# The sign of a float64 weight carried in the exponent through a parametric ReLU

## The chip, the cores and the metric

The program runs on one core of a Trainium2 chip. Its engines work side by side, each through its own queue in program order: TensorE (PE: matmuls, with PEld for the weight loads), VectorE (DVE), ScalarE (ACT), GpSimd (POOL), and SyncE (SP), which here issues DMA transfers. The metric is the device time of one execution in microseconds; lower is better.

## The reference

The program computes attention with a learned relative-position bias (2 x 8 heads, 576 positions, 64 wide), and then two dense blocks on the 1152 resulting rows of 512 numbers. Cut to what matters here:

```python
attn_out = _attn_ref(q, k, v, w1, b1, w2)
x = attn_out.transpose(0, 2, 1, 3).reshape(B * S, H * D)
h = x @ w_in                                   # block 1: 512 -> 2048
g = P(h) / (Q(h) + 1e-06)                      # P cubic, Q quadratic in |h|
x = g @ w_out                                  # 2048 -> 512
h = x @ w_in2                                  # block 2, other weights
g = where(h >= 1, h, where(h <= -1, 0, (h + 1)**2 / 4))
return (g @ w_out2).astype(float32)
```

The four weight matrices of the two blocks arrive as float64.

## The kernel before

PE multiplies fp32 numbers that are split in two: a high part (`wh`, `xh`, `gh`) and the remainder (`wl`, `xl`, `gl`), three matmuls for one product. So each float64 weight is turned into an fp32 word on the core, and that word into a high and a low part. This is `conv` (L475). It works on 64 tiles of 128 x 512 float64 numbers, 32 of queue k = 0 (the `w_in` side, pool `raw0`, results `wh` and `wl`) and 32 of queue k = 1 (the `w_out` side, pool `raw1`, result `wo`), in five stages, one per step:

- s0: `wc` = the high 32 bits, read as fp32, times 2^-112 (`copy`, L135 on ACT or L145 on POOL, whichever the planner takes).
- s1: two instructions. On ACT the top byte of the low word, shifted right by five bits through an arithmetic Copy on bytes, replaces the lowest byte of the high word in `raw` (L500; it is called the octet copy below). On DVE `wc` is shifted left by 3 bits (L501), which sets the exponent right and drops the sign.
- s2: DVE takes the sign and the low three bits from the high word in `raw` and joins them to `wc` (L504).
- s3: the next load into this `raw` buffer is issued on SP (`w_load`, L474; two buffers per queue, and the load waits until s2 has read the old content), and the high part is copied (L135 on ACT, L139 on DVE or L145 on POOL).
- s4: the low part is a subtraction on DVE or POOL (L150).

Four `wc` buffers rotate. Thirteen of the 64 conversions are placed in the attention stage, at steps that the table names (`ready0`: 27, 33, 37, 54, 69, 73; `ready1`: 59, 64, 67, 70, 73, 75, 77); the others stand in the dense blocks, eight for each twelve steps at first.

The order of the instructions is made when the program is built. A step is a row of operations with priorities; those that may run on several engines carry a cost for each, and `pick` (L100) gives each to the engine whose planned load stays lowest. So a changed cost or a removed choice moves other flexible operations too: the high-part copies, the first writes of `acc` (L139 or L135) and the additions into it, which run on DVE (L650) or as a copy to `dr` on ACT and an addition on POOL (L655).

In the attention stage a step holds the scores (L365, PE), their reduction with the bias (L374, DVE), the exponential (L379, ACT), the normalisation (L147, mostly POOL), transposes (L405, PE), their copies to `PT` (L135, ACT) and the product with V (L418 and L421, PE), from which `xh` (L438, ACT) and `xl` (L440, DVE) are made. In block 1 PE makes `inps` (L692), ACT and DVE turn it into `v` (L557 to L590), ACT and POOL split it into `gh` and `gl` (L594, L598), and nine steps later PE makes `outps` (L735). Between the blocks the sum `acc` is split into `x2h` (L667, ACT) and `x2l` (L668, DVE), which block 2 multiplies.

Of the kernel before, what the change touches and what calls it, by code (L numbers as in the profile page):

```python
# [8 lines left out]
AF = mybir.ActivationFunctionType  # L9
ALU = mybir.AluOpType  # L10
# [8 lines left out]
CH = 4  # L19
ADDC = 1.000001  # L20
I32 = mybir.dt.int32
U8 = mybir.dt.uint8

REBIAS = 2.0 ** -112

SIGN_LOW3 = -2147483648 + 7


def f(ap):
    return ap.bitcast(F32)  # L30
# [10 lines left out]
class Kernel:  # L41
# [436 lines left out]
    def conv(self, k):  # L478


        nc = self.nc
        p = self.wp[-1]
        q = self.wq[k]
        n = q["split"]
        q["split"] += 1
        self.w_load(k, n + 1)
        raw = q[n]
        words = raw.bitcast(I32).rearrange("p (n t) -> p n t", t=2)
        octets = raw.bitcast(U8).rearrange("p (n t) -> p n t", t=8)
        o = {}  # L490
        V, A, G = nc.vector, nc.scalar, nc.gpsimd
        tc = p.tile([128, 512], I32, tag="wc", name="wc", bufs=self.tbufs or 4)

        def s0():

            return [(dict(A=0.62, G=0.7), lambda e: self.copy(e, f(tc), f(raw).rearrange("p (n t) -> p n t", t=2)[:, :, 1], REBIAS))]

        def s1():

            return [(dict(A=0.62), lambda e: A.activation(octets[:, :, 4], octets[:, :, 3], AF.Copy, bias=-15.5 / 32, scale=1 / 32)),  # L500
                    (dict(V=0.34), lambda e: V.tensor_scalar(tc, tc, 3, None, ALU.logical_shift_left))]  # L501

        def s2():
            return [(dict(V=0.7), lambda e: V.scalar_tensor_tensor(tc, words[:, :, 1], SIGN_LOW3, tc, ALU.bitwise_and, ALU.bitwise_or))]  # L504

        def s3():
            self.w_load(k, n + 3)
            if k == 0:
                w = self.wp[n // 3 % 2]
                h = w.tile([128, 4, 128], F32R, tag="wh", name="wh", bufs=3)  # L510
                l = w.tile([128, 4, 128], F32R, tag="wl", name="wl", bufs=3)
                hf, lf = h.rearrange("p a b -> p (a b)"), l.rearrange("p a b -> p (a b)")
            else:
                t = self.ring("wo")
                hf, lf = t[:, 0:512], t[:, 512:1024]
                h, l = (y.rearrange("p (a b) -> p a b", a=4) for y in (hf, lf))
            q[n] = (h, l)
            o["hf"], o["lf"] = hf, lf
            return [(dict(A=0.6, V=0.34, G=0.64), lambda e: self.copy(e, hf, f(tc)))]

        def s4():
            return [(dict(V=0.6, G=1.23), lambda e: self.sub(e, o["lf"], f(tc), f(o["hf"])))]

        return [s0, s1, s2, s3, s4]

    def conv_at(self, k, s):
# [350 lines left out]
```

## Time and profile before

| what | value |
|---|---|
| median of 3 runs | 630.74 us (629.16 to 631.07) |
| profiled execution, device time | 633.58 us |
| its span in the trace | 631.8 us |
| mean granted TensorE clock | 0.988 of full speed |
| PE busy | 593.3 us (94%) |
| DVE busy | 540.0 us (85%) |
| ACT busy | 457.9 us (72%) |
| POOL busy | 430.6 us (68%) |

The profiled execution is 2.84 us above the median, and its device time is 1.8 us more than the span of its instructions. Busy shares are means over three stages: attention to about 226 us, block 1 to about 415 us, block 2 to the end.

### The profile page before, as it was taken

What the parts mean: (1) busy time and instruction counts of PE and PEld (TensorE: products, weight loads), DVE (VectorE), ACT (ScalarE), POOL (GpSimd) and SP (SyncE); (2) the same over time, 40 slices, a digit from 0 to 9 for tenths busy, and PEclk for the clock granted to TensorE, in tenths of its full rate; (3) what the DMA queues carried; (4) which work ended last, traced back from release to release, by engine and by line L of the source; (5) the groups of instructions that cost most, each with busy time, mean ns of one, the idle gap of its engine ahead of it and who ended that gap; (6) DMA issues with size and microseconds to landing.
All of it is one profiled execution on the core that took longest, in us unless ns stands there. A gap on an engine that the chain in (4) does not pass through costs nothing.

```text
span 631.8 us, 11439 instructions
## 1 busy us (share of the span) xinstructions
PE 593.3 (94%) x4084; PEld 539.4 (85%) x4084; DVE 540.0 (85%) x984; ACT 457.9 (72%) x901; POOL 430.6 (68%) x454
## 2 busy tenths in 40 slices
PE   4679999999988879999999999989999999999997
PEld 1147777677877769999999999989999999999997
DVE  7998898999669779989999999999999599696432
ACT  4478787888789779999799879967666555474330
POOL 5957667686769557888899979776576466475220
PEclk9999999999999979999999999989999999999999
DMA  6956335664554311222122221233132132010012
GB/s 209 245 146 215 111 115 187 223 219 155 153 193 148 110 34 35 66 71 98 67 95 73 67 72 64 67 100 101 34 133 101 34 116 107 13 67 1 13 51 87
DMA packets 26888, 66.26 MB, mean 105 GB/s; under 512 B 4688, under 2 KB 6608, under 8 KB 26832
## 3 DMA queue, kind: packets, MB, share of 16 engines
q1 hardware_dynamic: 26688, 65.44, 32.3%
q8 instruction: 32, 0.52, 0.4%
q14 instruction: 24, 0.20, 0.1%
q10 hardware_dynamic: 144, 0.10, 0.1%
HBM read 51.19 MB, written 9.62 MB: 96 GB/s over the span
## 4 chain that ended last, share of the span: by engine, by line
PE 42%; DVE 19%; ACT 5%; issue 0%; POOL 0%; ACTq 0%
PE outps L735 22%; PE inps L692 20%; DVE wc L504 3%; DVE wc L501 2%; DVE v L571 2%; DVE inps L589 2%; DVE v L572 2%; DVE v L590 2%; DVE q L588 2%; DVE acc L650 1%; ACT raw L500 1%; ACT v L559 1%; ACT q L558 1%; ACT h L557 1%; DVE wh L139 1%; DVE wo L139 1%
## 5 line engine op out<-in xcount | busy, mean ns | idle before, releaser
L735 PE MATMUL outps<-gh,wo 128*128 128x384 f32 x768 | 210.8, 337 | 0.2 <-DVE acc L650 0.2
L598 POOL TENSOR_TENSOR gl<-v,gh 128x384 fp32r<-128x384 f32 x96 | 109.0, 1135 | 87.8 <-ACT gh L594 79.7
L735 PEld LDWEIGHTS outps<-gh,wo 128*128 128x128 f32 x768 | 140.9, 189 | 0.5 <-DVE acc L650 0.5
L735 PE MATMUL outps<-gl,wo 128*128 128x384 f32 x384 | 128.8, 335 | 0.0
L692 PE MATMUL inps<-x,wh 128*128 128x384 f32 x384 | 100.7, 343 | 6.4 <-DVE x L440 4.9
L500 ACT ACTIVATE raw<-raw 128x512 uint8<-128x512 uint8 x64 | 86.4, 1385 | 0.0
L147 POOL TENSOR_SCALAR P<-P,m 128x576 f32<-128x576 f32 x72 | 59.9, 835 | 32.8 <-DVE m L384 23.3
L594 ACT ACTIVATE gh<-v 128x384 fp32r<-128x384 f32 x96 | 50.6, 527 | 43.4 <-DVE v L586 43.1
L692 PEld LDWEIGHTS inps<-x,wh 128*128 128x128 f32 x384 | 70.7, 192 | 7.7 <-DVE x L440 5.2
L735 PEld LDWEIGHTS outps<-gl,wo 128*128 128x128 f32 x384 | 72.6, 189 | 0.0
L379 ACT ACTIVATE P<-P,m 128x576 f32<-128x576 f32 x72 | 56.0, 778 | 17.9 <-DVE m L374 17.8
L365 PE MATMUL sps<-K,Q 128*128 128x288 f32 x320 | 61.0, 317 | 6.6 <-DVE m L374 6.6
L692 PE MATMUL inps<-x2h,wh 128*128 128x384 f32 x192 | 64.6, 337 | 2.1 <-ACT x2h L667 2.1
L692 PE MATMUL inps<-x,wl 128*128 128x384 f32 x192 | 65.5, 341 | 0.0
L692 PE MATMUL inps<-x2l,wh 128*128 128x384 f32 x192 | 64.6, 336 | 0.2 <-DVE x2l L668 0.2
L692 PE MATMUL inps<-x2h,wl 128*128 128x384 f32 x192 | 64.7, 337 | 0.0
L220 PE MATMUL bps<-hid,w2s 128*32 128x288 f32 (+17 forms) x416 | 48.7, 468 | 15.7 <-DVE hid L209 14.7
L374 DVE CUSTOM_DVE_ANT_0 P<-sps,bias 128x576 f32<-128x576 f32 x72 | 53.3, 748 | 10.9 <-DMA bias<-bd 7.9
L504 DVE SCALAR_TENSOR_TENSOR wc<-raw,wc 128x512 int32<-128x512 int32 x64 | 62.4, 985 | 0.1
L565 POOL TENSOR_TENSOR q<-h,q 128x384 f32<-128x384 f32 x48 | 49.7, 1035 | 18.7 <-ACT q L558 18.7
L501 DVE TENSOR_SCALAR wc<-wc 128x512 int32<-128x512 int32 x64 | 57.6, 908 | 0.7 <-ACT wc L135 0.7
L365 PEld LDWEIGHTS sps<-K,Q 128*128 128x128 f32 x320 | 45.7, 192 | 11.0 <-DVE m L374 5.9
(89 smaller groups left out, 1337.4 us busy)
## 6 DMA issues: line engine op xcount, KB each, us to landing
raw<-w SPq DMA_DIRECT2D x64, 512.0 KB
bd<-bbuf SPq DMA_DIRECT2D x24, 295.5 KB
bias<-bd SPq DMA_DIRECT2D x24, 288.0 KB
bias<-bbuf SPq DMA_DIRECT2D x16, 288.0 KB
qraw<-qm SPq DMA_DIRECT2D x16, 256.0 KB
V<-v SPq DMA_DIRECT2D x8, 320.0 KB
kraw<-kc SPq DMA_DIRECT2D x4, 576.0 KB
out<-acc SPq DMA_DIRECT2D x12, 192.0 KB
```

The costliest lines, as they stand in the source:

```text
L147: nc.gpsimd.tensor_scalar(out, x, scale, 1.0, ALU.mult, ALU.mult)
L365: PE.matmul(x_[:, x, :288], lhsT=lhs, rhs=K[h][:, bb, 288 * x:288 * x + 288], start=(j == 0), stop=(j == len(seq) - 1))
L374: V.tensor_tensor_reduce(halves(o), S_.pop(t)[:, :, :288], halves(bt), -0.125, 3e38, ALU.add, ALU.min, sums[i][:, 0, e:e + 1])
L379: A.activation(s, s, AF.Exp, bias=m[:, 0, e:e + 1], scale=-1.0, accum_out=m[:, 1, e:e + 1])
L500: return [(dict(A=0.62), lambda e: A.activation(octets[:, :, 4], octets[:, :, 3], AF.Copy, bias=-15.5 / 32, scale=1 / 32)), (dict(V=0.34), ...
L501: (dict(V=0.34), lambda e: V.tensor_scalar(tc, tc, 3, None, ALU.logical_shift_left))]
L504: return [(dict(V=0.7), lambda e: V.scalar_tensor_tensor(tc, words[:, :, 1], SIGN_LOW3, tc, ALU.bitwise_and, ALU.bitwise_or))]
L565: return [lambda: G.tensor_tensor(o["q"], o["h2"], o["q"], ALU.add)] if m == 0 else []
L594: return [lambda: A.activation(gh, o["v"], AF.Copy)]
L598: return [lambda: G.tensor_tensor(gl, o["v"], f(o["gh"]), ALU.subtract)]
L692: nc.tensor.matmul(ps[:, :U], lhsT=w[:, c], rhs=y[:, c], start=(t == 0), stop=(t == 11))
L735: nc.tensor.matmul(ps[:, :U], lhsT=w[:, c], rhs=y, start=(t == 0), stop=(t == 11))
```

## The change

Stage s0 becomes one ACT instruction: a parametric ReLU of the high word with scale 2^-112, in which negative numbers are multiplied by a further 2^32. That adds 32 to the exponent of negative numbers alone, and the bit it sets is the one that the shift by 3 moves to the sign's place. The octet copy goes, and so does POOL's choice for s0. Stage s2 stays one DVE instruction of the same kind, but reads the low word of `raw`, shifted right by 29, in place of the high word with a mask. `raw` is no longer written by the core.

```diff
-SIGN_LOW3 = -2147483648 + 7
+NEGATIVE = 2.0 ** 32
...
-            return [(dict(A=0.62, G=0.7), lambda e: self.copy(e, f(tc), f(raw).rearrange("p (n t) -> p n t", t=2)[:, :, 1], REBIAS))]
+            x = f(raw).rearrange("p (n t) -> p n t", t=2)[:, :, 1]
+            return [(dict(A=0.62), lambda e: A.activation(f(tc), x, AF.Prelu, scale=REBIAS, alpha=NEGATIVE))]
...
-            return [(dict(A=0.62), lambda e: A.activation(octets[:, :, 4], octets[:, :, 3], AF.Copy, bias=-15.5 / 32, scale=1 / 32)),
-                    (dict(V=0.34), lambda e: V.tensor_scalar(tc, tc, 3, None, ALU.logical_shift_left))]
+            return [(dict(V=0.34), lambda e: V.tensor_scalar(tc, tc, 3, None, ALU.logical_shift_left))]
...
-            return [(dict(V=0.7), lambda e: V.scalar_tensor_tensor(tc, words[:, :, 1], SIGN_LOW3, tc, ALU.bitwise_and, ALU.bitwise_or))]
+            return [(dict(V=0.7), lambda e: V.scalar_tensor_tensor(tc, words[:, :, 0], 29, tc, ALU.logical_shift_right, ALU.bitwise_or))]
```

The order on PE and on SP stays the same, instruction by instruction. On ACT, DVE and POOL it changes, and two places are shown. The first is the end of the attention stage, on ACT, before the change: from the last exponential to the first operation of block 1 on the numbers of its first matmul (`raw_2371` is a tile of queue k = 0, the other three are of k = 1; `x` is the high part that goes into block 1).

```order
L379 ACTIVATE P,m<-P,m 128x576
L135 ACTIVATE PT<-tps 128x384 x2
L500 ACTIVATE raw_2371<-raw_2371 128x512
L500 ACTIVATE raw_2731<-raw_2731 128x512
L135 ACTIVATE PT<-tps 128x384
L438 ACTIVATE x_1249<-vps 128x256
L500 ACTIVATE raw_2824<-raw_2824 128x512
L135 ACTIVATE wc<-raw_2901 128x512
L500 ACTIVATE raw_2901<-raw_2901 128x512
L557 ACTIVATE h_2997<-inps,sb_1475 128x384
```

Rows that only copy further transposes to `PT` are left out above and below. The same place with the change (line numbers fall by one or two; the four tiles are the same ones under other buffer numbers, 2367, 2724, 2815 and 2890):

```order
L378 ACTIVATE P,m<-P,m 128x576
L495 ACTIVATE wc<-raw_2367 128x512
L495 ACTIVATE wc<-raw_2724 128x512
L134 ACTIVATE PT<-tps 128x384 x3
L437 ACTIVATE x_1249<-vps 128x256
L495 ACTIVATE wc<-raw_2815 128x512
L495 ACTIVATE wc<-raw_2890 128x512
L134 ACTIVATE PT<-tps 128x384 x2
L555 ACTIVATE h_2984<-inps,sb_1474 128x384
```

The four octet copies are gone, the last of them from right ahead of `h`; the first three tiles have their s0 here on ACT, where it stood on POOL, and one step ahead of where the octet copy stood.

The second place is the change from block 1 to block 2, on POOL: the operations ahead of the last addition into the first column group of `acc`, which `x2h` reads. Before:

```order
L598 TENSOR_TENSOR gl<-v,gh 128x384
L150 TENSOR_TENSOR wl<-wc,wh 128x512
L598 TENSOR_TENSOR gl<-v,gh 128x384
L145 TENSOR_SCALAR wc<-raw_5168 128x512
L655 TENSOR_TENSOR acc<-acc,dr 128x384
```

With the change:

```order
L596 TENSOR_TENSOR gl<-v,gh 128x384
L149 TENSOR_TENSOR wl<-wc,wh 128x512
L596 TENSOR_TENSOR gl<-v,gh 128x384
L653 TENSOR_TENSOR acc<-acc,dr 128x384
L144 TENSOR_SCALAR wo<-wc 128x512
```

The copy of s0 between `gl` and the addition is gone, and a high-part copy stands behind the addition. On ACT the octet copy that stood right ahead of the copy to `dr` gives its place to a parametric ReLU.

Over the whole program ACT loses 64 octet copies, 12 copies of s0 and 7 high-part copies and gets 64 parametric ReLUs, 3 copies to `acc` and 3 to `dr`; POOL loses 52 copies of s0 and gets 22 high-part copies and 3 additions; DVE loses 15 high-part copies, 3 copies to `acc` and 3 additions.

## Rows read from the trace of the kernel before

**Rows 1.** Stretches: busy us of PE, PEld, DVE, ACT, POOL; PEclk, DMA share, GB/s

```profile
95.00:205.00 110.00, 103.62 (x992) 81.16 (x988) 93.36 (x239) 93.45 (x221) 82.96 (x106) 1.00 0.56 182
205.00:226.00 21.00, 14.45 (x117) 12.73 (x116) 17.19 (x30) 17.18 (x31) 11.84 (x11) 0.96 0.33 114
242.00:395.00 153.00, 152.48 (x875) 152.12 (x874) 149.75 (x260) 139.83 (x260) 135.21 (x131) 1.00 0.22 73
395.00:420.00 25.00, 22.61 (x118) 21.72 (x118) 24.08 (x43) 21.45 (x39) 17.70 (x17) 0.93 0.26 85
420.00:630.00 210.00, 208.43 (x1197) 208.11 (x1195) 160.35 (x226) 110.94 (x193) 110.91 (x96) 1.00 0.19 66
```

**Rows 2.** What PE waited for: us in total, times, longest us

```profile
PE vps L418 <- ACT PT L135: 3.5, 2, 1.9
PE inps L692 <- ACT x2h L667: 2.1, 1, 2.1
```

**Rows 3.** Groups of instructions: busy us, mean ns, idle before and its releasers

```profile
L500 ACT ACTIVATE raw<-raw 128x512 uint8<-128x512 uint8 x64 | 86.4, 1385 | 0.0
L135 ACT ACTIVATE wc<-raw 128x512 f32<-128x512 f32 x12 | 8.0, 671 | 4.7 <-DVE wo L139 3.1 <-POOL wo L150 1.5
L145 POOL TENSOR_SCALAR wc<-raw 128x512 f32<-128x512 f32 x52 | 42.9, 827 | 0.5 <-DMA raw<-w 0.2
L52 ACT ACT_TABLE_LOAD x1 | 1.3, 1283 | 0.7 <-PEq L870 0.7
```

**Rows 4.** The shift on DVE: count, duration ns min/median/max

```profile
L501 DVE TENSOR_SCALAR wc<-wc x64: 411/1036/1523, 103.4 to 573.3; 128x512 int32<-128x512 int32 x64
```

**Rows 5.** ACT in order of time, 193 to 202 us

```profile
193.67 1.36 ACT L500 ACTIVATE raw<-raw 128x512 uint8<-128x512 uint8 x1
...
200.11 1.35 ACT L500 ACTIVATE raw<-raw 128x512 uint8<-128x512 uint8 x1
201.19 0.96 ACT L135 ACTIVATE PT<-tps 128x384 f32<-128x384 f32 x2
```

**Rows 6.** DVE in order of time, 204 to 210 us

```profile
204.77 0.87 DVE L139 CAST wo<-wc 128x512 fp32r<-128x512 f32 x1
...
207.88 1.75 DVE L504 SCALAR_TENSOR_TENSOR wc<-raw,wc 128x512 int32<-128x512 int32 x2
```

**Rows 7.** SP's issues of weight loads, 208 to 211 us

```profile
209.05 0.93 SPq L474 DMA_DIRECT2D raw<-w  x2
```

**Rows 8.** ACT in order of time, 210 to 217 us

```profile
213.91 0.66 ACT L135 ACTIVATE wc<-raw 128x512 f32<-128x512 f32 x1 [3.11 <-DVE wo L139]
214.47 0.86 ACT L135 ACTIVATE PT<-tps 128x384 f32<-128x384 f32 x2
215.21 1.36 ACT L500 ACTIVATE raw<-raw 128x512 uint8<-128x512 uint8 x1
216.30 0.59 ACT L557 ACTIVATE h<-inps,sb 128x384 f32<-128x384 f32 x1
```

**Rows 9.** PE in order of time, where it restarts after a gap

```profile
225.82 1.01 PE L692 MATMUL inps<-x,wh 128*128 128x384 f32 x2 [4.88 <-DVE x L440]
...
239.98 0.62 PE L692 MATMUL inps<-x,wh 128*128 128x384 f32 x2 [0.95 <-DVE v L590]
```

**Rows 10.** Two stretches behind PE's gaps, columns as in rows 1

```profile
226.00:231.00 5.00, 5.00 (x16) 5.00 (x17) 2.67 (x6) 1.41 (x4) 1.01 (x1) 0.50 0.01 3
415.00:420.00 5.00, 4.86 (x19) 4.86 (x20) 4.96 (x9) 3.20 (x5) 2.69 (x2) 0.66 0.33 111
```

**Rows 11.** ACT in order of time, 410 to 415 us

```profile
410.55 1.36 ACT L500 ACTIVATE raw<-raw 128x512 uint8<-128x512 uint8 x1
411.65 0.58 ACT L135 ACTIVATE dr<-outps 128x384 f32<-128x384 f32 x1
```

**Rows 12.** POOL in order of time, 410 to 414 us

```profile
411.71 1.10 POOL L145 TENSOR_SCALAR wc<-raw 128x512 f32<-128x512 f32 x1
412.78 1.16 POOL L655 TENSOR_TENSOR acc<-acc,dr 128x384 f32<-128x384 f32 x1
```

More of the change, by code (lines that the diff above doesn't have):

```diff
@@ L21 @@
 I32 = mybir.dt.int32
-U8 = mybir.dt.uint8
 REBIAS = 2.0 ** -112
-SIGN_LOW3 = -2147483648 + 7
+NEGATIVE = 2.0 ** 32
 def f(ap):
@@ L488, in conv @@
         words = raw.bitcast(I32).rearrange("p (n t) -> p n t", t=2)
-        octets = raw.bitcast(U8).rearrange("p (n t) -> p n t", t=8)
         o = {}
```

## The prediction

> **What bounds the kernel now.** I read the stretches first [rows 1]. From 242 to 395 us and from 420 to 630 us PE is busy for 152.48 of 153 and 208.43 of 210 us at full granted clock, and these two stretches are over half of the run. An engine that is relieved there buys nothing, as long as it stays ahead of PE: ACT was busy for 139.83 of 153 us in the first and 110.94 of 210 in the second. The conversions, 64 in all, mostly stand in these two stretches. So the 86.4 us of the octet copy [rows 3] are not a saving to be taken over.
>
> What can be saved lies where PE stands still or runs slowly after the first conversion: 95 to 205 us (PE idle 6.4 us), 205 to 226 us (6.55 us), and 395 to 420 us (2.4 us, with a mean granted clock of 0.93) [rows 1]. The chain of waits of PE says for two of these gaps what ended them: `PT` copies on ACT, up to 1.9 us at once, and `x2h` on ACT, 2.1 us [rows 2]. The longest gap, 4.88 us, ends at 225.82 us with `xl` [rows 9]. All three stand behind conversions. Of the other idle time I count nothing.
>
> **The change part by part.** Price of the new instruction: the trace has no parametric ReLU. The nearest row is the Copy of the same words on the same engine, 671 ns [rows 3]; the other end is the octet copy, 1385 ns, equally 512 elements long. Its scale, bias and slope are constants of the instruction as in the Copy, so I take 671 ns. Below that nothing on ACT of this size speaks. ACT then loses 64 x 1.385 + 12 x 0.671 = 96.7 us and gets 64 x 0.671 = 42.9 us; POOL loses 52 x 0.827 = 43.0 us of s0 [rows 3] and gets back 22 high-part copies; DVE loses 15 of them. None of this counts by itself; I go through the gaps.
>
> *End of attention, first half.* Three octet copies stand on ACT from 193.67 us to the `PT` copies that start at 201.19 us [rows 5]. Each takes its place from start to next start, 200.11 to 201.19 = 1.08 us, so 3.2 us in all. With the change two parametric ReLUs stand there (the order on ACT), each for 214.47 - 213.91 = 0.56 us [rows 8], 1.1 us. So ACT comes to `PT` 2.1 us earlier, and the PE gap of 1.9 us [rows 2] closes but for what the transposes themselves need. I take 1.6 us; bounds 0 (something else is late then) and 1.9.
>
> *End of attention, second half.* ACT waits 3.11 us for the s0 copy that starts at 213.91 us [rows 8]. The view names a DVE copy, but that copy doesn't write what is read; what is read is the tile whose load SP issued in the pair from 209.05 to 209.98 us [rows 7], so I take the load for the releaser, 3.9 us after its issue. The load waits for L504 of the tile two before, one of the two that run from 207.88 us on [rows 6]. DVE gets there earlier by the 1.6 us above, and by the high-part copy at 204.77 us, 0.87 us [rows 6], which goes to POOL; I take 0.8. So the load lands, and the s0 behind it starts, 2.4 us earlier. Then the octet copy at 215.21 us is gone, which held `h` from 215.21 to 216.30 = 1.1 us [rows 8]. `h` starts the serial chain of block 1 on ACT and DVE in whose queue `xl` stands, and the order of both from there on is unchanged. So PE restarts 1.6 + 0.8 + 1.1 = **3.5 us** earlier than at 225.82 us. Bounds: 1.1 if the load doesn't move, 3.5 and what DVE gains by a quieter POOL.
>
> For that last point, the shift on DVE takes from 411 to 1523 ns for one shape [rows 4]. The Trainium skill ("SBUF — State Buffer", Who interferes with whom) says that DVE in its two-port modes and GpSimd take turns at one pair of ports, the loser waiting for the whole instruction. The spread agrees with that rule. By it fewer POOL copies shorten the two shifts ahead of L504; from the median to the shortest that would be 2 x 0.625 = 1.25 us more, and the sum below 8.0 us. But the change also puts 22 copies on POOL, and I count nothing.
>
> *After the restart.* PE waits 0.95 us at 239.98 us [rows 9] for DVE, behind ACT, where an octet copy stands just ahead. A parametric ReLU one step earlier takes half of its time: **0.5 us**; bounds 0 and 0.95.
>
> *Block 1, 242 to 395 us, and block 2.* Nothing: PE is the cover, 152.48 of 153 us. If that cover went, ACT's queue would have to be late by more than the 13.2 us that it was idle there [rows 1].
>
> *From block 1 to block 2.* The last sum for the first columns goes `dr` on ACT, addition on POOL, `x2h` on ACT. `dr` starts at 411.65 us behind an octet copy [rows 11], and the addition starts at 412.78 us behind a POOL copy that began at 411.71 us [rows 12]. With the change a ReLU 0.5 us shorter in step stands ahead of `dr`, and nothing ahead of the addition. It starts when `dr` is done, 411.65 - 0.5 + 0.58 = 411.73 us, so 1.0 us earlier. PE's gap of 2.1 us [rows 2] falls to about 1.1. Behind it the granted clock was 0.66 of full speed over 5 us [rows 10], that is part of the stretch at the lower of the two levels, 1.2 GHz; this costs 0.34 x 5 = 1.7 us. In the stretch of 95 to 205 us the clock stayed at 1.00 [rows 1] although PE stood still for 1.9 us in it [rows 2], so I take the clock to stay up after 1.1 us: **2.7 us** together; bounds 0 and 3.2.
>
> After the restart at 225.82 us, 5 us ran at 0.50 [rows 10], a loss of 2.5 us. The gap in front of it shrinks only as far as its end moves more than its start; the start moves with the `PT` copies by 2.4 us, the end by 3.5, so about 3.8 us stay and I leave that loss as it is.
>
> **The sum.** 3.5 + 0.5 + 2.7 = 6.7 us. The profiled execution took 633.58 us and would take 626.9; it lies 2.84 us above the median of the runs, so the median would be **624.0 us**. What a measurement of this kernel can tell from no change is about 0.3%, 1.9 us.
>
> **The rivals.**
>
> *The clock holds at the restart too.* If the gap in front of 225.82 us becomes short enough, the 2.5 us of rows 10 come on top: 621.5. For it: the bounds of a quieter POOL. Against it: 3.8 us are left by the sum, twice the 1.9 us that went without a fall.
>
> *The chains are held by something else.* The load at the end of attention lands when it did, because DVE, busy for 17.19 of 21 us there [rows 1], comes to L504 no sooner, and `x2h` is late for another reason. Then 1.1 + 0.5 us are left: 629.1, no change that can be told. For it: PE's wait at the restart is named after DVE, and DVE's order there is nearly the old one.
>
> *The new instruction blocks ACT.* All 64 now stand in ACT's queue and wait there for their load and for a free `wc`, one step ahead of the octet copy; behind them are the exponentials, `PT`, `dr`. Of the 12 copies that stood on ACT so far, two waited, 4.7 us together [rows 3], 0.39 us each; the 52 on POOL held only POOL. At that rate the 13 conversions of the attention stage hold ACT for 5.1 us on the path, and the one ahead of `dr` for 1.5 us; the 1.1 + 0.5 us of the last rival stay as a gain: +5.0 us, 635.7. It decides for slower when more than 6.7 + 1.9 us of such waits fall on the path. Against it: the 52 copies on POOL had 0.5 us of idle time ahead of them in all [rows 3], so loads and buffers were mostly there in time.
>
> *The function isn't in the loaded table.* One table load takes 1283 ns [rows 3]; a pair for each of the 64 would put 164 us on ACT, 13 pairs or 33 us of it on the attention path: some 664 us. The Trainium skill ("ScalarE: Activation LUTs", Table sets: the hidden batching unit) says that functions of different sets cost a load at each switch. By that rule it would apply only where a load stands in the order, and the changed program has the one at its start, so I give it 1 in 100.
>
> **How the numbers follow.** The forecast has 0.55, its own range 621 to 627 (the bounds of the first half of the gap and of the transition between the blocks). The clock at the restart 0.15; held by something else 0.18; ACT blocked 0.11; table loads 0.01. So faster 0.70, same 0.18, slower 0.12. The range goes from 620 (the second case with some of the DVE time) to 631, which leaves out the last two cases and the ends.
>
> **What would show it.** In the profile after: L495 at about 670 ns x64; ACT busy down by some 55 us and POOL by 20 to 30; PE's wait at 201 us gone, its restart at about 222 us, the wait for `x2h` about 1 us with a clock of 1.00 behind it; PE busy shares in 242 to 395 us as now. Wrong it would be if L495 shows waits of microseconds ahead of `PT` or `dr`, if the instruction takes over 1 us, or if PE's restart keeps its distance to the landing of the last load while that load doesn't move.

## The result, and the profile after

The kernel after the change takes 624.55 us (median of 4 runs, 623.83 to 625.17), beside 630.9 us for the kernel before (4 runs, 629.16 to 631.58): 0.9903 of it, 95% interval 0.9879 to 0.9927. It is faster, and the forecast of 624.0 us was 0.55 us off. Run twice more, on other chips, it gave 0.9874 (0.9844 to 0.9904) and 0.9910 (0.9889 to 0.9931).

The page of the kernel after: busy time of each engine.

```profile
PE 590.9 (95%) x4084; PEld 538.0 (87%) x4084; DVE 514.9 (83%) x963; ACT 411.5 (66%) x888; POOL 408.1 (66%) x427
```

ACT is busy for 46.4 us less than before, POOL for 22.5 and DVE for 25.1; of these 94 us, some 6 reached the end of the program. The groups of instructions in the kernel after:

```profile
L498 DVE TENSOR_SCALAR wc<-wc 128x512 int32<-128x512 int32 x64 | 47.3, 748 | 1.4 <-ACT wc L495 1.4
L495 ACT ACTIVATE wc<-raw 128x512 f32<-128x512 f32 x64 | 42.3, 672 | 9.2 <-POOL wo L149 4.7 <-DMA raw<-w 4.3
L51 ACT ACT_TABLE_LOAD x1 | 1.3, 1283 | 0.7 <-PEq L868 0.7
```

The parametric ReLU takes 672 ns, as the Copy did [rows 3], and no second table load came with it. But ACT now waits 9.2 us ahead of L495. The stretches, columns as in [rows 1]:

```profile
95.00:205.00 110.00, 105.97 (x1016) 83.56 (x1017) 95.08 (x243) 90.56 (x224) 78.74 (x97) 1.00 0.55 182
205.00:226.00 21.00, 17.31 (x99) 16.04 (x96) 15.48 (x30) 14.03 (x30) 9.07 (x9) 0.84 0.27 99
242.00:395.00 153.00, 153.00 (x880) 153.00 (x879) 136.58 (x257) 124.84 (x258) 125.28 (x122) 1.00 0.21 73
395.00:420.00 25.00, 24.12 (x138) 23.70 (x137) 23.96 (x35) 13.45 (x28) 16.14 (x14) 1.00 0.30 99
```

The stretch from 242 to 395 us stayed full (block 2, the other full one, is the last column of the table below), and PE's 2.4 us of idle time in the passage between the blocks shrank to 0.9 us with the clock at 1.00. Around the end of attention the mean clock is lower than before, 0.84. PE in order of time, where it had to wait there, first of before and then of after; the last row of after is PE's wait in the passage:

```profile
201.82 0.49 PE L418 MATMUL vps<-PT,V 128*128 128x128 f32 x2 [1.87 <-ACT PT L135]
...
215.00 0.49 PE L418 MATMUL vps<-PT,V 128*128 128x128 f32 x2 [1.67 <-ACT PT L135]
```

```profile
204.14 0.49 PE L417 MATMUL vps<-PT,V 128*128 128x128 f32 x2 [0.51 <-ACT PT L134]
...
210.24 0.49 PE L417 MATMUL vps<-PT,V 128*128 128x128 f32 x2 [1.67 <-ACT PT L134]
...
219.77 0.62 PE L690 MATMUL inps<-x,wh 128*128 128x384 f32 x2 [2.02 <-DVE x L439]
...
233.31 0.62 PE L690 MATMUL inps<-x,wh 128*128 128x384 f32 x2 [1.28 <-DVE v L588]
...
405.68 0.44 PE L690 MATMUL inps<-x2l,wh 128*128 128x384 f32 x1 [0.88 <-DVE x2l L666]
```

The 1.87 us gap that ended at 201.82 us in before is gone (the 0.51 us at 204.14 stand ahead of a later product). The gap of 1.67 us that ended at 215.00 is still there, at 210.24, and the restart (the product of block 1 that stands behind PE's longest gap in before) waits 2.02 instead of 4.88 us [rows 9]. What holds the second gap is seen on ACT, in order of time (after):

```profile
203.02 0.69 ACT L495 ACTIVATE wc<-raw 128x512 f32<-128x512 f32 x1
203.61 1.24 ACT L134 ACTIVATE PT<-tps 128x384 f32<-128x384 f32 x3
209.14 0.66 ACT L495 ACTIVATE wc<-raw 128x512 f32<-128x512 f32 x1 [4.30 <-DMA raw<-w]
209.70 0.86 ACT L134 ACTIVATE PT<-tps 128x384 f32<-128x384 f32 x2
210.44 0.59 ACT L555 ACTIVATE h<-inps,sb 128x384 f32<-128x384 f32 x1
```

The ReLU at 209.14 us waits 4.30 us for its load, and the two `PT` copies wait in the queue behind it; `h` comes right after them, with no octet copy between [rows 8].

**A yardstick.** TensorE issues the same 4084 instructions in the same order in every kernel below, so the time between the same two of them can be compared. I take the starts of four instructions, those at 188.84, 242.19, 406.82 and 439.50 us of before, and the last one at 628.10. The first is the score product behind the last long wait for a bias; the next intervals are the end of attention with the restart, block 1, and the passage to block 2. The table is worked out from these starts in one profiled execution of each kernel:

```
                              start   end of     block 1  passage  rest
                                      attention
before                        188.84  53.35      164.63   32.68    188.60
after                         185.51  50.02      163.76   30.21    188.60
after, second chip            186.71  51.47      163.76   30.22    188.60
after, third chip             187.28  50.99      163.76   30.22    188.60
octets left out               188.50  50.90      164.43   31.93    188.60
octets put back               185.51  53.28      163.95   30.81    188.60
copies all on ACT             187.40  54.72      163.92   31.19    188.60
octet priced 1.3              188.35  54.59      164.13   33.97    188.59
new form in attention only    185.90  50.45      164.13   32.49    188.60
new form in experts only      186.72  53.89      163.77   30.25    188.60
last conversion later         185.10  50.81      163.77   30.21    188.60
low half earlier              187.72  48.27      163.77   30.24    188.60
both moved                    187.52  47.20      163.77   30.23    188.60
both moved, another chip      185.10  47.34      163.76   30.23    188.60
```

Three executions of the kernel after agree within 0.01 us in the last three columns and within 1.5 us in the end of attention; before the first mark they differ by 1.8 us. With the mean of the three, the change gave 2.5 us at the end of attention, 0.9 in block 1 and 2.5 in the passage, 5.9 us together; the medians of the three comparisons differ by 6.35, 6.67 and 5.92 us. Of before there is a single profile, so a difference in the column of the end of attention that rests on one pair of profiles is known to about 1.5 us; up to the restart the three of after agree within 0.3. What lies before the first mark (3.3 us between before and the first profile of after) is not much more than the 2.4 us by which the two profiles of both moves differ there, and I claim none of it.

### The profile page after: what moved, and what is told of

Read it like the earlier page. It is cut to its first block, busy times and chain, and to the rows that moved or that the text cites. A ratio compares the mean times of both kernels' runs of the same rounds, so it can differ in the third digit from the quotient of the medians.

```text
span 621.8 us, 11331 instructions
## 1 busy us (share of the span) xinstructions
PE 590.9 (95%) x4084; PEld 538.0 (87%) x4084; DVE 514.9 (83%) x963; ACT 411.5 (66%) x888; POOL 408.1 (66%) x427
## 4 chain that ended last, share of the span: by engine, by line
PE 71%; DVE 16%; DMA 6%; issue 2%; ACT 2%; POOL 0%; SPq 0%; DVEq 0%; ACTq 0%; POOLq 0%
PE outps L733 30%; PE inps L690 29%; DVE hid L208 5%; PE tps L404 3%; PE vps L420 3%; PE sps L364 3%; PE bps L219 3%; DMA bias<-bd 3%; DVE P L373 2%; DVE wc L498 2%; DMA raw<-w 1%; DVE wc L502 1%; DVE K L149 1%; DMA qraw<-qt 1%; PE vps L417 1%
## 5 line engine op out<-in xcount | busy, mean ns | idle before, releaser
L559 ACT ACTIVATE v<-inps,cst 128x384 f32<-128x384 f32 x48 | 27.8, 579 | 66.4 <-PE inps L690 63.5
L583 DVE SCALAR_TENSOR_TENSOR v<-v 128x384 f32<-128x384 f32 x48 | 39.8, 829 | 33.9 <-ACT v L559 33.6
L502 DVE SCALAR_TENSOR_TENSOR wc<-raw,wc 128x512 int32<-128x512 int32 x64 | 61.3, 968 | 0.0
```

The source lines that it names most:

```text
L583: return [lambda: V.scalar_tensor_tensor(v, v, 1.0, v, ALU.min, ALU.mult), lambda: V.tensor_tensor(v, v, h2, ALU.add)]
```

## The experiments

Three theories: ScalarE's time in the octet copies was the loss (1); GpSimd's scaled copies, which run beside VectorE's shifts, were it (2); the plan's new order was it (3). The first four runs shared one chip, where before took 631.58 us.

**The octet copy left out of the kernel before, in its order**

```diff
-            return [(dict(A=0.62), lambda e: A.activation(octets[:, :, 4], octets[:, :, 3], AF.Copy, bias=-15.5 / 32, scale=1 / 32)),
+            return [(dict(A=0.62), lambda e: None),
```

> The kernel before with the 64 octet copies of ScalarE left out, and every engine's other instructions in the order that they had (so the sign and the three low bits of each weight are wrong and nothing else; 52 scaled copies stay on GpSimd). Theory 1, ScalarE's time in the octet copies is what the two chains lost: the end of attention gives 2.7 us (1.6 of the gap at 201 and 1.1 of the octet ahead of h; the cast of 0.8 stays on VectorE), the transition between the blocks 0 to 2.7 (the octet ahead of dr goes, GpSimd's copy ahead of the sum stays), so 625.5 to 628.2 against 630.9. Theory 2, GpSimd's copies and VectorE's shifts that they slow are the cause: 630.9, within 0.8. Theory 3, the new order of the work is the cause: 630.9 too.

Measured: 629.36 us, 0.9971 (0.9953 to 0.9989). That is 1.2 us above theory 1's range (by the gain on this chip, 2.2 us, it misses the least of 2.7 by 0.5) and outside theories 2 and 3. In the table the passage gave 0.75 of the possible 2.7 us. The end of attention gave 2.45 us in this one profile, near theory 1's 2.7; but the medians leave only 1.3 us for all that lies ahead of block 1. ACT and POOL between the blocks, in order of time (kernel without the octet copies):

```profile
407.02 0.47 ACT L135 ACTIVATE dr<-outps 128x384 f32<-128x384 f32 x1
...
410.42 0.52 ACT L667 ACTIVATE x2h<-acc 128x384 fp32r<-128x384 f32 x1 [2.04 <-POOL acc L655]
```

```profile
407.19 1.02 POOL L598 TENSOR_TENSOR gl<-v,gh 128x384 fp32r<-128x384 f32 x1 [1.56 <-ACT gh L594]
408.18 1.09 POOL L145 TENSOR_SCALAR wc<-raw 128x512 f32<-128x512 f32 x1
409.22 1.17 POOL L655 TENSOR_TENSOR acc<-acc,dr 128x384 f32<-128x384 f32 x1
```

`dr` is there at 407.5 us, but the addition starts at 409.22, behind a scaled copy of 1.09 us on POOL, and `x2h` waits for it. Here it was GpSimd that held PE.

**The octet copy put back into the kernel after, in its order**

```diff
+            octets = raw.bitcast(mybir.dt.uint8).rearrange("p (n t) -> p n t", t=8)
+            return [(dict(A=0.0), lambda e: A.activation(octets[:, :, 4], octets[:, :, 3], AF.Copy, bias=-15.5 / 32, scale=1 / 32)),
+                    (dict(V=0.34), lambda e: V.tensor_scalar(tc, tc, 3, None, ALU.logical_shift_left))]
```

> The kernel after with the octet copies put back on ScalarE, with no cost in the plan, so that every engine's other instructions keep the order of after; nobody reads the byte that they write. Theory 1: the octets' time comes back on both chains, 2.7 us at the end of attention and 1 to 2.7 at the transition, so 628 to 630 against 630.9 of before and 624.55 of after. Theory 2 (GpSimd relieved, VectorE's shifts shorter): 624.5, as after. Theory 3 (the order): 624.5.

Measured: 628.54 us, 0.9961 (0.9944 to 0.9977): inside theory 1's 628 to 630. The end of attention is back at 53.28 us, the passage only at 30.81. PE's gap is back where before had it (PE in order of time, octets put back):

```profile
199.57 0.49 PE L417 MATMUL vps<-PT,V 128*128 128x128 f32 x2 [1.97 <-ACT PT L134]
```

**All scaled copies on ScalarE, octets kept**

```diff
-            return [(dict(A=0.62, G=0.7), lambda e: self.copy(e, f(tc), ..., REBIAS))]
+            return [(dict(A=0.62), lambda e: self.copy(e, f(tc), ..., REBIAS))]
```

> The kernel before with all 64 scaled copies on ScalarE (none on GpSimd), the octet copies kept. ScalarE gets 52 x 671 ns = 35 us more, GpSimd 52 x 827 ns = 43 us less. Theory 1: nothing is gained at the end of attention, where ScalarE is what TensorE waits for; 631 to 634. Theory 2: VectorE's shifts fall to some 460 ns as in after, and the gain comes without the octets' leaving: 625 to 628. Theory 3: between, by what the plan moves, 628 to 632.

Measured: 631.53 us, 0.9997 (0.9986 to 1.0007), no change: inside theory 1's range (631 to 634) and theory 3's (628 to 632), not theory 2's. But it is no change made of two: the passage and block 1 gave 1.5 and 0.7 us, and as the total is unchanged, what lies ahead of block 1 took about as much back (1.4 us at the end of attention in the one profile). Theory 2 is right in the passage and wrong at the end of attention.

**The octet copy at its real price in the plan**

```diff
-            return [(dict(A=0.62), ...octet copy...
+            return [(dict(A=1.3), ...octet copy...
```

> The kernel before with one number changed: the plan counts an octet copy at 1.3 instead of 0.62, near what it takes (1385 ns), so that the plan orders the other work of ScalarE around it; the instructions themselves are the same. Theory 3, the order is what cost the time: 626 to 628. Theories 1 and 2: the octets still take 86 us of ScalarE and GpSimd still makes scaled copies; 629.5 to 632.

Measured: 633.91 us, 1.0037 (1.0025 to 1.005). That is slower than before and outside the range of every theory. With the right price the plan's order lost 1.2 us at the end of attention and 1.3 in the passage. Why that order is worse I did not follow up. So an order alone can cost 2.3 us. The first two runs, each in its kernel's own order, show that the order is not the whole of the gain; but no run has the order of after with the scaled copies still on GpSimd, and what that order gave by itself stays open.

**The new form in one part of the conversions alone.** Both runs, the next one and the kernel after again were on one chip, where before took 631.89 us.

```diff
+        prelu = at          # in the other kernel: not at
...
+            if prelu:
+                return [(dict(A=0.62), lambda e: A.activation(f(tc), x, AF.Prelu, scale=REBIAS, alpha=NEGATIVE))]
+            return [(dict(A=0.62, G=0.7), lambda e: self.copy(e, f(tc), x, REBIAS))]
...
-                st["f"] = self.conv(k)
+                st["f"] = self.conv(k, True)
```

> The new form in the 13 conversions under attention alone; the 51 under the expert stages keep the old one. If the gain is two local chains, as predicted, this has the end of attention (3.5 us, less the 0.3 that the product after the restart lost) and not the transition: 627.5 to 628.5 where before has 631.2. If one place carries it all, 624.5 or 631.

> The reverse: the old form in the 13 conversions under attention, the new one in the 51 under the expert stages. Two local chains: the transition's 2.7 us alone, 628 to 629. If one place carries it all: 631 or 624.5; the two gains of this pair should add up to that of the whole change, 6.2.

Measured: 627.91 us, 0.9927 (0.9904 to 0.9951), and 628.9 us, 0.995 (0.9931 to 0.997), both as two local chains have it. The differences, 4.0 and 3.0 us, add up to 7.0, beside 6.67 for the whole change on the same chip. In the table the gain of the 13 under attention stands at the end of attention (2.9 us, and 0.5 in block 1), that of the 51 in block 1 and the passage (0.9 and 2.4). PE's gap for `x2h`, and the clock around it, with the new form under attention only:

```profile
408.22 0.44 PE L700 MATMUL inps<-x2h,wh 128*128 128x384 f32 x1 [2.07 <-ACT x2h L675]
```

```profile
395.00:420.00 25.00, 22.60 (x127) 21.72 (x126) 23.64 (x38) 19.48 (x33) 17.38 (x17) 1.00 0.27 87
```

The gap is the one of before [rows 2], but the clock is 1.00 and not 0.93 [rows 1]; ACT, DVE and POOL have the order of before in this passage, and still it takes 32.49 us, only 0.2 less. PE waits once more for `x2h`, where before does not:

```profile
426.36 0.44 PE L700 MATMUL inps<-x2h,wh 128*128 128x384 f32 x1 [0.66 <-ACT x2h L675]
```

And with the new form in the experts only, PE at the same place:

```profile
410.78 0.44 PE L700 MATMUL inps<-x2l,wh 128*128 128x384 f32 x1 [0.88 <-DVE x2l L676]
```

Nothing waits for `x2h` any more; 0.88 us for `x2l` is left.

**What holds the end of attention now**

```diff
-    'ready1': [59, 64, 67, 70, 73, 75, 77]
+    'ready1': [59, 64, 67, 70, 73, 75, 78]
```

> The kernel after with the last conversion under attention planned one step later (78 for 77), which puts its parametric ReLU, which waits 4.30 us for its load at 209.14, behind the two PT evacuations that stood behind it. If that wait is what is left at the end of attention, the gap of 1.67 us at 210.24 closes and the clock does not fall after it: 1.5 to 3 us faster than after on the same chip, 621.5 to 623. If the low half of x, for which TensorE waits 2.02 us at the restart, is what holds the chain, it is moved by nothing here: as after, 624 to 625.

> The kernel after, unchanged, on the chip of the three others, as their measure: 0.988 to 0.993 of before, 623.5 to 626.

Measured: 625.51 us, 0.9895 (0.9866 to 0.9923), beside 625.22 us for after (0.9874, just below the ratio that was expected of it). The gap closed as the edit was meant to make it, but the 1.5 to 3 us did not come: no difference that can be told. PE and VectorE in order of time (last conversion later):

```profile
204.10 0.49 PE L417 MATMUL vps<-PT,V 128*128 128x128 f32 x2 [0.79 <-ACT PT L134]
...
219.17 1.01 PE L690 MATMUL inps<-x,wh 128*128 128x384 f32 x2 [4.96 <-DVE x L439]
```

```profile
218.24 0.54 DVE L588 SCALAR_TENSOR_TENSOR v<-q,inps 128x384 f32<-128x384 f32 x1
218.70 0.41 DVE L439 TENSOR_TENSOR x<-vps,x 128x256 fp32r<-128x256 f32 x1
```

PE no longer waits for the last `PT`, works ahead, and stands 4.96 us at the restart instead. L439 makes the low half of the last piece of `x`; its inputs were there some 6 us earlier, but it stands in VectorE's queue behind the `v` of three tiles. So that place was moved:

```diff
-                    at(2 * i + PAR["xl"], "V", lambda y=y: out(1, *y), PAR["vp"][4])
+                    at(2 * i + (9 if i == len(pairs) - 1 else PAR["xl"]), "V", lambda y=y: out(1, *y), PAR["vp"][4])
```

> The last conversion one step later, and besides the low half of the last piece of x, for which TensorE waits 4.96 us at the restart, taken up by VectorE right behind its first squares and not behind the v of three tiles (one instruction moved up ten places, nothing else). Its inputs are there at 212.8 in the run with the later conversion alone, and TensorE comes to it at 214.1. If the restart is held by that place in VectorE's order alone, the gap of 4.96 us closes and the half clock behind it goes: 4 to 7 us faster than after, 618 to 621. If TensorE then waits for the elementwise chain a few tiles on instead (v, for which it waits 1.28 us at 233 to 236), part comes back: 621 to 623.5. If nothing changes, the restart was held by something that the trace does not name: 625.

> The second of the two moves alone, on the kernel after: the low half earlier, the last conversion where it was. The wait of 1.6 us for PT stays and the restart's 2 to 3.8 us go: 2 to 4 us faster than after, 621 to 623; if the chain further on takes it back, 624 to 625.

Measured, where before took 631.58 us: both moves 622.45 us, 0.9849 (0.9826 to 0.9871), the second branch of the expectation (part comes back); the low half alone 623.07 us, 0.9859 (0.9836 to 0.9882), just above the 621 to 623 of its first branch. Then both moves and the kernel after side by side, before at 631.39 us:

> The kernel with both moves again, now beside after on one chip, since their intervals, 0.9826 to 0.9871 of before and 0.9844 to 0.9904, overlap. If the 5 us at the restart are given back by 2.5 to 3 us of waits for v behind it, as the trace of the first run shows, 0.983 to 0.987 of before, and 2 to 3 us below after. If the difference was the chip's, both at 0.987 to 0.990.

> The kernel after, on the same chip as the kernel with both moves: 0.987 to 0.990 of before, whichever theory holds.

Measured: 621.21 us, 0.9841 (0.9817 to 0.9866), and 625.47 us, 0.9910 (0.9889 to 0.9931). The intervals do not meet: the two moves gain 4.3 us more on this chip, above the 2 to 3 that were expected (after itself, at 0.9910, came out just above its 0.987 to 0.990), and this is the fastest version. VectorE and PE in order of time, and two stretches (both moved, the second run):

```profile
211.60 0.62 DVE L570 SCALAR_TENSOR_TENSOR v<-v,abn,inps 128x384 f32<-128x384 f32 x1
212.79 0.42 DVE L439 TENSOR_TENSOR x<-vps,x 128x256 fp32r<-128x256 f32 x1 [0.58 <-ACT x L437]
```

```profile
218.85 0.61 PE L690 MATMUL inps<-x,wh 128*128 128x384 f32 x2 [3.03 <-DVE v L588]
```

```profile
205.00:218.00 13.00, 10.82 (x74) 10.17 (x72) 9.38 (x17) 9.89 (x20) 5.58 (x6) 1.00 0.37 120
218.00:226.00 8.00, 6.41 (x33) 5.77 (x34) 8.00 (x17) 7.52 (x16) 5.18 (x6) 1.00 0.12 49
```

L439 now waits for its own input (0.58 us), the wait at the restart is gone, and PE stands 3.03 us a few products later, for the elementwise `v` on VectorE. VectorE works there without a pause: from 212.79 us, through that wait, and for 8.00 of the 8 us from 218. That makes it the likely limit now; no run moved it.

## Why the prediction was right, step by step

**Price.** 671 ns was taken, 672 measured. ACT's busy time fell by 46 us, where some 55 were named as a sign. The rival of table loads went with the single one in the program.

**The sum.** 6.7 us were forecast, 6.35 measured, and that it came this close is in part luck: the end of attention and the product behind the restart gave 1.5 us less than forecast (2.5 instead of 4.0), block 1 seemed to give 0.9 that were counted at nothing, and the passage came right from two terms that were both wrong.

**End of attention, first half: the step that was too large.** That the PE gap of 1.9 us closes held: it is gone. That VectorE therefore reaches the merge (stage s2, L504 in before and L502 in after) ahead of the load 1.6 us earlier did not. In before VectorE waited for PE just ahead of that part:

```profile
203.38 0.42 DVE L440 TENSOR_TENSOR x<-vps,x 128x256 fp32r<-128x256 f32 x1 [0.34 <-PE vps L421]
203.72 1.13 DVE L150 TENSOR_TENSOR wl<-wc,wh 128x512 fp32r<-128x512 f32 x1
```

and in after the same pair follows other work with no wait:

```profile
199.40 0.41 DVE L439 TENSOR_TENSOR x<-vps,x 128x256 fp32r<-128x256 f32 x1
199.74 0.99 DVE L149 TENSOR_TENSOR wl<-wc,wh 128x512 fp32r<-128x512 f32 x1
...
202.94 1.74 DVE L502 SCALAR_TENSOR_TENSOR wc<-raw,wc 128x512 int32<-128x512 int32 x2
```

Measured from the first mark of each, the subtraction `wl` starts 14.88 us after it in before and 14.23 in after: 0.65 us came through, and then VectorE itself was the limit. From `wl` to the two merges it was 4.16 us and is 3.20: the 0.8 us of the high-part copy that went to POOL are there (0.96). Together the merges come 1.6 us earlier and not 2.4, and the landing of the load by 25.07 - 23.63 = 1.4 us.

**Second half.** The octet copy ahead of `h`, 1.1 us: held. From the first mark to the restart it was 36.98 us, and is 34.26, 34.57 and 34.49 in the three profiles of after, so 2.4 to 2.7 us instead of 3.5; less the 1.4 of the load, 1.0 to 1.3 are left for the octet. That the octets count here is shown from both sides, but not that they carry the stage alone. Put back, they cost the restart at least 2.4 us (37.02 us from the first mark). Left out of before's order, they gave it 1.4 (35.55 us): the octet ahead of `h`, and nothing of the load, for which ACT then stands longer (octets left out):

```profile
213.44 0.66 ACT L135 ACTIVATE wc<-raw 128x512 f32<-128x512 f32 x1 [5.53 <-DMA raw<-w]
```

That is 24.9 us after the first mark, beside 25.1 in before. The other 1.0 us of the 2.45 in the table lie behind the restart (15.35 us to 242.19, beside 16.37), where one kernel's profiles differ by 1.1. So the 1.4 us of the load also need what VectorE gained by the high-part copy or by the new order.

**After the restart, 0.5 us: not there.** From the restart to 242.19 us it was 16.37 us, and is 15.76, 16.90 and 16.50. PE's wait grew from 0.95 to 1.28 us. The octet copy stood just ahead of that wait, but it was not on the path: ACT took it up behind the `v` that VectorE needs next. The ReLU, one step earlier, stands ahead of `h`, `q` and that `v`, and VectorE now waits 0.85 us for it, 0.29 before (ACT and DVE in order of time, after):

```profile
228.23 0.68 ACT L495 ACTIVATE wc<-raw 128x512 f32<-128x512 f32 x1
230.12 0.70 ACT L557 ACTIVATE v<-inps,abn 128x384 f32<-128x384 f32 x1
```

```profile
230.85 0.55 DVE L569 TENSOR_TENSOR v<-v,inps 128x384 f32<-128x384 f32 x1 [0.85 <-ACT v L557]
```

The other runs sort the same way: PE's wait is 0.89 to 0.96 us in the four kernels with this s0 on POOL (before, octets left out, octet priced, new form in attention only) and 1.27 to 1.36 in those with it on ACT, octets or not, but for the two runs with both moves (1.06 and 1.09).

**The restart's clock.** "About 3.8 us stay and I leave that loss as it is": the two later profiles of after have gaps of 3.81 and 3.80 us, and in the second chip's run the 6 us from the restart ran at 0.50:

```profile
221.00:227.00 6.00, 5.72 (x18) 5.72 (x19) 3.13 (x7) 2.40 (x6) 1.36 (x2) 0.50 0.01 3
```

In the first profile the gap was 2.02 us only because PE itself was late: 210 to 214 us ran at 0.60; behind it, 221 to 224 us still ran at 0.50.

**Block 1, nothing: 0.9 us.** A small miss. PE's 0.5 us of idle time in 242 to 395 us [rows 1] is gone. With the copies off POOL, octets or not, the block takes 163.8 to 164.0 us; with the octets alone left out, 164.43. But it takes 164.13 with the new form under attention only, where ACT, DVE and POOL have before's order and instructions in this block. So 0.5 of the 0.9 us also go without any change in the block; 0.2 to 0.4 are left that POOL's relief, which I had counted at nothing, may have given.

**The passage, 2.7 us: 2.5 measured, but the split was wrong.** I gave 1.0 us to the chain and 1.7 to the clock. With the new form under attention alone the clock stayed up behind an unchanged gap, and the passage took 32.49 us, not 31. From the product behind the gap to the end of the passage it is 24.95 us in before, 0.15 of it waits, and 24.75 here, 0.96 of it waits (0.66 the next one for `x2h`, the rest short ones). So the clock cost PE some 1.0 us and not 1.7, and all but 0.2 of that had been hidden by the chain behind. The gain is the chain's: some 0.7 us from the octets alone (31.93) and 1.5 from moving the copies off POOL alone (31.19), 2.5 from both. That POOL's copy ahead of the addition counts was right; its price was too low.

**The rivals.** The blocked ACT is real, but on one load: the wait for `PT` behind it is 1.67 us, and it stood in before as well. The other 4.7 us that ACT waits ahead of L495 fall at 408.54 and 502.77 us, and PE waits for ACT behind neither. (The 1.5 us that this rival put ahead of `dr` do not follow from its rate of 0.39 us for each; at that rate it is 0.4, and the rival's time 634.6 us.) Chains held by something else: no. The clock at the restart came only with the two moves (218 to 226 us at 1.00), not with the change.

**VectorE's shifts.** The Trainium skill ("SBUF — State Buffer", Who interferes with whom) says that VectorE, in its two-port modes, and GpSimd take turns at a shared pair of ports; by it, fewer GpSimd copies make the shifts shorter. The trace agrees: the mean shift took 908 ns before, 748 after, 881 with only the octets gone and 790 with only the copies gone. But the stage in which the prediction weighed it did not gain by that: with the copies alone moved, the end of attention took 54.72 us, no less than the 53.35 of before.

## What to carry to other kernels

Taking 94 us of work off three engines gave 6 us, and reading the two chains on which that work stood ahead of something TensorE waited for told how much; but follow each engine on the chain by itself, since one that has its own backlog hands on only part of an earlier start. Undo each half of a change apart: here one half won mostly in one stage and the other in another, and one of them alone, the copies' move, was worth nothing. When a wait closes and the time stays, look for the same time at the next wait of the same engine; here two moves in the order, one of them of a single instruction, were worth 4 us more.

## What the runs showed of the hardware

- The granted clock did not follow the length of the last gap. It fell to 0.60 over the 4 us behind a gap of 1.67 us in after, and to 0.50 behind 3.81 us; it stayed at 1.00 behind 3.03 us with both moves, and behind 2.07 us at the passage with the new form under attention only. Even ahead of the same product it went either way: 1.00 over the 4 us behind 1.67 us in before (215 to 219 us) and behind 1.58 us in the second chip's run of after (211 to 215 us). What else decides is open.
- A lost clock need not cost its loss: 1.7 us by the granted clock at the passage of before were some 1.0 us of PE's time and worth about 0.2 us of the passage, as the chain behind was the later one.
- From the issue of the weight load that ACT waits for at the end of attention to the s0 that reads it, 4.26 us passed in before (209.65 to 213.91) and 4.38 in after (204.76 to 209.14); in the fourteen profiles it is 4.26 to 4.71. No change on the engines made this piece of the chain shorter.
